# A new fixed order of attention, weight decoding and first MLP, with no tensor operation on GpSimd

## Chip, core and metric

The kernel runs on one core of one Trainium2 chip. The metric is the device time of one execution in microseconds (us), as the median of several runs; less is better. The profiles are of one execution each, taken by the hardware profiler, and times within it count from the span's start.

## What is computed

Chunked attention, an MLP with a swish, and a mixture of eight experts with one expert for each token, all in float32, on 2 x 768 tokens of 512 dimensions. Cut to what matters:

```python
for c in range(nc):                       # chunks of 32 queries
    k_full = concat([mem_k, k[:, :, l_start:r_end]])   # 8 + up to 56 keys
    a = exp(s - max(s)); a = a / (a.sum(-1) + 1e-9)    # s = scale * q_c @ k_full.T
    out[:, :, c_start:c_end] = a @ v_full
h = x @ w_in                              # first MLP: 512 -> 2048 -> 512
x = (h / (1 + exp(-1.702 * h))) @ w_out
logits = x @ w_gate                       # second: the best of 8 experts
y = relu(x_e @ w1[e]) @ w2[e]             # at most 384 tokens of each, 512 -> 1024 -> 512
out = gate_w * y
```

The weights of the first MLP come in 64 bits. The kernel decodes them from pairs of 32-bit words.

## The kernel before

Tokens are in 12 groups of 128, two groups to a block of the first MLP. All products of the MLPs are made from values split in a high and a low part, with three matmuls for each product (high by high, high by low, low by high).

The first part of the program is issued in an order written out by hand, the string ORDER. Each word is a step, a letter and a number. The scheduler keeps this order on each engine (`in_order`), and an engine's instruction that waits holds all behind it on that engine. The last step of the string is followed by a loop over the rest of the first MLP with the routing, and then by the experts. Those two parts are generated by the program and scheduled by priorities.

Steps of a group g of attention: Q, K, V load (SyncE's queue; two buffers each); c makes the scores (TensorE, 64 small matmuls, line 424); m the maximum (VectorE, 444); s the difference (VectorE, 451); x the exponential (ScalarE, 456), X that of two groups at once; r the sum (VectorE, 460); q adds a small number (463) and i takes the reciprocal (466, both VectorE); n divides on VectorE, N on GpSimd (470); d transposes (TensorE, 477); p copies with zeros beside (ScalarE, 485); e multiplies with the values (TensorE, 494); h and l write the high part (ScalarE, 506) and the low part (VectorE, 509) of xT, the input of the first MLP.

Steps of a piece of weights p (32 pieces of 128 x 512; in each eight, four of w_in, then four of w_out): L loads its raw words (SyncE, three buffers, line 938); a takes the absolute value of the high words (ScalarE, 254); b limits it (258), f shifts it (261), o sets the sign (265, all VectorE); t converts the low words on ScalarE (273), T on VectorE (275); g adds the two on GpSimd, G on VectorE (279); w makes the high part (ScalarE, 284); j the low part on VectorE, J on GpSimd (289).

Steps of a unit u of the first MLP (96 units; one is a block of 256 tokens by 128 hidden columns): A makes the hidden values (TensorE, 12 matmuls, 528) into one of two PSUM buffers; z and y apply the swish twice (ScalarE, 543 and 547), which frees the buffer; u makes the low part on VectorE, U on GpSimd (551); B multiplies with w_out (TensorE, 6 matmuls, 571) into two accumulators; v adds a finished accumulator to x2 (VectorE, 584; the first twelve are copied by ScalarE, 587). Units run in four passes over the hidden columns, four columns' chunks in a pass, and within a pass over the six blocks of tokens. U1 = 74 says that ORDER holds the units below 74.

F is a number of matmuls without use, which keep the tensor engine's clock up (line 929). E ends attention: it gives back its memory.

Of the kernel before, what the change touches and what calls it, by code (L numbers as in the profile page):

```python
# [54 lines left out]
i4 z4 b8 y4 r5 N4 w6 u4 B1 z5 q5 j6 i5 m7 N5 A6 y5 f8 s7 u5 A7 o8 X7 T7 T8 c8 L10 G7 L11 r6 z6 T9 d4 a9 K10 q6
m8 d5 z7 Q10 p4 c9 r7 s8 p5 G8 B2 Q11 m9 a10 K11 w8 T10 e4 s9 w7 j8 y6 J7 b10 e5 V6 q7 f10 i7 U6 o10 X9 B3 i6
V7 G10 N6 h5 n7 h4 c10 r8 v1 v0 l4 q8 l5 d6 B4 i8 m10 y7 p6 b9 U7 n8 A8 w10 f9 r9 a11 J10 A9 o9 z8 y8 b11 L12
g9 q9 i9 A10 L13 f11 z9 o11 U8 w9 B5 t11 N9 j9 z10 L14 g11 d7 y9 d8 t12 s10 A11 p7 u9 a12 e6 z11 b12 t13 f12
a13 B6 o12 V8 a14 b13 L15 h6 b14 w11 B7 l6 y10 j11 p8 U10 e7 f14 f13 y11 v3 o14 U11 v2 e8 G12 V9 h7 o13 w12 l7
B8 a15 V10 j12 h8 L16 G13 A12 l8 w13 T14 t15 A13 j13 L17 z12 y12 G14 U12 b15 A14 w14 f15 z13 j14 d9 o15 t16 B9  # L60
a16 L18 G15 p9 b16 B10 T17 f16 y13 z14 U13 o16 w15 e9 a17 L19 G16 y14 j15 a18 A15 b17 V11 h9 b18 t18 f17 f18
B11 z15 o17 o18 L20 g17 a19 c11 l9 L21 v4 y15 b19 g18 v5 T19 f19 A16 u15 m11 A17 o19 t20 u14 L22 g19 s11 z16
B12 z17 T21 B13 X11 B14 r10 r11 B15 y16 q10 y17 i10 q11 U16 i11 u17 N10 A18 v6 v7 N11 d10 z18 B16 y18 p10 U18
d11 e10 p11 A19 h10 l10 e11 z19 y19 U19 B17 h11 l11 B18 E0 w16 w17 j16 w18 A20 j17 w19 a20 j18 J19 B19 a21 b20
z20 b21 y20 f20 a22 A21 U20 f21 v8 b22 v9 o21 A22 f22 z21 g21 y21 o20 o22 L23 A23 z22 g20 L24 y22 u22 A24 U21
T22 w20 L25 G22 w21 z23 j20 B20 J21 z24 y23 t23 a23 A25 U23 y24 b23 w22 U24 T24 a24 A26 f23 J22 o23 z25 a25
b24 L26 B21 g23 f24 z26 b25 o24 B22 w23 f25 L27 G24 y25 t25 u25 B23 y26 o25 U26 a26 T26 L28 j23 g25 A27 v11
b26 v10 f26 w24 T27 A28 o26 z27 J24 y27 a27 L29 G26 A29 w25 b27 U27 t28 f27 J25 z28 o27 B24 a28 z29 L30 b28
w26 g27 f28 B25 y28 o28 a29 J26 T29 w27 L31 A30 u28 y29 b29 u29 f29 A31 j27 a30 G28 z30 b30 B26 t30 o29 z31
a31 f30 g29 B27 o30 y30 b31 U30 T31 A32 v12 y31 g30 v13 A33 f31 z32 U31 o31 G31 B28 z33 B29 y32 U32 A34 y33  # L70
U33 A35 z34 B30 z35 B31 y34 u34 A36 v14 y35 v15 A37 u35 z36 B32 z37 B33 y36 u36 A38 y37 U37 A39 z38 B34 z39
B35 y38 u38 A40 v17 y39 U39 v16 A41 z40 B36 z41 B37 y40 u40 B38 y41 u41 A42 A43 z42 y42 U42 B39 z43 A44 v19
y43 v18 A45 u43 z44 B40 z45 B41 y44 U44 A46 y45 u45 A47 z46 B42 z47 w28 w29 J28 B43 y46 w30 u46 w31 J29 A48
v21 y47 v20 J31 A49 z48 J30 B44 U47 B45 y48 z49 U48 A50 y49 U49 A51 z50 B46 z51 B47 y50 u50 A52 v23 y51 u51
# [1124 lines left out]
```

## Time and profile before

| | |
|---|---|
| time, median of 3 runs | 566.86 us (565.52 to 567.95) |
| the profiled execution: its span, first to last instruction | 564.0 us |
| its span below the median of the runs | 2.9 us |
| TensorE matmul busy | 525.7 us, 93% of the span |
| VectorE | 309.0 us, 55% |
| ScalarE | 272.1 us, 48% |
| GpSimd | 139.0 us, 25% |
| mean granted clock of TensorE | 0.979 of full speed |

Of the profiled execution the page gives the span alone; the runs of the table are other executions. The engines PE, PEld, DVE, ACT, POOL and SP of the profile are TensorE's matmuls, its weight loads, VectorE, ScalarE, GpSimd and SyncE. A busy share is a mean over parts of the program that are bound by different engines. A duration is from start to end of an instruction; successive instructions of an engine can overlap a little, so the distance of starts is the pace.

### The profile page before, as it was taken

How to read it: one execution, taken by the hardware profiler on the slowest of the kernel's cores; microseconds unless marked ns; L12 is line 12 of the kernel's file. 1: busy time of each engine (PE TensorE's matmuls, PEld its weight loads, DVE VectorE, ACT ScalarE, POOL GpSimd, SP SyncE). 2: the span in 40 equal slices, each digit the busy share in tenths (PEclk: the TensorE clock that was granted, in tenths of full speed). 3: DMA queues.
4: the chain of work that ended last, by engine and by line, in shares of the span. 5: the costliest groups of instructions: out<-in, count | busy, mean ns of one | idle time of the engine just before them, and what ended most of it. 6: DMA issues, size and time to landing. Idle time of an engine off the chain costs nothing.

```text
span 564.0 us, 10773 instructions
## 1 busy us (share of the span) xinstructions
PE 525.7 (93%) x4266; PEld 452.3 (80%) x4272; DVE 309.0 (55%) x580; ACT 272.1 (48%) x543; POOL 139.0 (25%) x147
## 2 busy tenths in 40 slices
PE   8599799999699999999999999939999999999995
PEld 4498578797588989898998888528998898899894
DVE  4999999669962111212237344525846082975350
ACT  3588977766532242222145333216654282956250
POOL 3543341537540050201100000150040214302011
PEclk9889999999899999999999999969999999999998
DMA  8857756304450000000028511386957165895100
GB/s 322 321 180 266 248 170 230 127 21 151 134 181 0 1 1 1 1 1 0 1 71 279 175 39 40 114 277 215 299 178 266 58 205 184 275 371 184 72 26 29
DMA packets 39036, 80.57 MB, mean 143 GB/s; under 512 B 4025, under 2 KB 10169, under 8 KB 38970
## 3 DMA queue, kind: packets, MB, share of 16 engines
q1 hardware_dynamic: 36010, 70.66, 37.1%
q0 software_dynamic: 2960, 9.01, 5.1%
q8 instruction: 44, 0.72, 0.5%
q14 instruction: 22, 0.18, 0.1%
HBM read 70.16 MB, written 10.27 MB: 143 GB/s over the span
## 4 chain that ended last, share of the span: by engine, by line
PE 56%; DVE 17%; issue 13%; DMA 7%; ACT 5%; POOL 1%; POOLq 0%; SPq 0%; ACTq 0%
PE acc L571 18%; PE psh L528 17%; PE psy L816 8%; PE psh L750 6%; DVE w L258 3%; DVE w L265 3%; DMA out_dram<-y,taker 2%; DVE w L289 2%; PE psh L772 2%; DVE w L261 2%; DMA out_dram<-y,tl 2%; DVE rest L275 1%; DMA kt<-in_k_dram 1%; PE psr L598 1%; DVE xT L509 1%
## 5 line engine op out<-in xcount | busy, mean ns | idle before, releaser
L528 PE MATMUL psh<-xT,w 128*128 128x256 f32 x1152 | 153.1, 287 | 14.2 <-ACT g L547 7.5
L528 PEld LDWEIGHTS psh<-xT,w 128*128 128x128 f32 x1152 | 146.6, 193 | 22.1 <-ACT g L547 10.1
L571 PE MATMUL acc<-w,g 128*128 128x512 f32 x576 | 148.0, 400 | 2.5 <-DVE x L584 0.9
L571 PEld LDWEIGHTS acc<-w,g 128*128 128x128 f32 x576 | 103.4, 188 | 25.9 <-issue 2.1
L289 DVE TENSOR_TENSOR w<-raw,w 128x1024 fp32r<-128x1024 f32 x64 | 77.1, 1217 | 48.9 <-ACT w L284 48.7
L816 PE MATMUL psy<-w,hT 128*128 128x512 f32 x360 | 87.5, 398 | 0.3 <-ACT y L836 0.3
L543 ACT ACTIVATE sg<-psh 128x256 f32<-128x256 f32 x96 | 36.7, 383 | 100.2 <-PE psh L528 95.8
L551 DVE TENSOR_TENSOR g<-sg,g 128x256 fp32r<-128x256 f32 x57 | 28.1, 494 | 99.6 <-ACT g L547 92.7
L816 PEld LDWEIGHTS psy<-w,hT 128*128 128x128 f32 x360 | 66.5, 188 | 16.3 <-ACT y L836 0.6
L750 PEld LDWEIGHTS psh<-xs,w 128*128 128x128 f32 x576 | 69.0, 188 | 0.6
L750 PE MATMUL psh<-xs,w 128*128 128x256 f32 x576 | 69.2, 281 | 0.0
L284 ACT ACTIVATE w<-raw 128x1024 fp32r<-128x1024 f32 x64 | 66.4, 1062 | 0.0
L551 POOL TENSOR_TENSOR g<-sg,g 128x256 fp32r<-128x256 f32 x39 | 32.8, 841 | 114.4 <-ACT g L547 109.6
L547 ACT ACTIVATE g<-psh 128x256 fp32r<-128x256 f32 x96 | 36.6, 382 | 35.3 <-PE acc L571 35.1
L699 POOL DMA_INDIRECT xr<-rows,taker x22 | 26.7, 1216 | 98.3 <-issue 97.5
L584 DVE SCALAR_TENSOR_TENSOR x<-acc,x 128x512 f32<-128x512 f32 x36 | 23.5, 684 | 25.5 <-PE acc L571 25.5
L279 POOL TENSOR_TENSOR w<-w,rest 128x512 int32<-128x512 int32 x17 | 24.7, 1458 | 28.4 <-DVE w L265 27.4
L837 POOL DMA_INDIRECT out_dram<-y,taker x7 | 7.0, 1004 | 92.1 <-ACTq L854 71.9
L289 POOL TENSOR_TENSOR w<-w,w 128x512 fp32r<-128x512 f32 x16 | 22.5, 1413 | 26.4 <-ACT w L284 25.9
L265 DVE SCALAR_TENSOR_TENSOR w<-raw,w 128x512 int32<-128x512 int32 x32 | 26.9, 852 | 0.3
L284 ACT ACTIVATE w<-w 128x512 fp32r<-128x512 f32 x32 | 19.4, 627 | 12.3 <-POOL w L279 8.1
L772 PE MATMUL psh<-w,xs 128*128 128x512 f32 x72 | 19.4, 421 | 5.8 <-issue 5.8
(108 smaller groups left out, 503.2 us busy)
## 6 DMA issues: line engine op xcount, KB each, us to landing
raw<-in_w_dram SPq DMA_DIRECT2D x64, 512.0 KB, 5.8
raw<-in_w_in_dram SPq DMA_DIRECT2D x16, 512.0 KB, 4.2
raw<-in_w_out_dram SPq DMA_DIRECT2D x16, 512.0 KB, 3.6
vt<-in_v_dram SPq DMA_DIRECT2D x12, 512.0 KB, 6.2
...
```

What stands on the lines that cost most here:

```text
L265: nc.vector.scalar_tensor_tensor(out=self.w, in0=self.words()[1], scalar=-0x40000000, in1=self.w, op0=ALU.bitwise_and, op1=ALU.bitwise_or)
L284: nc.scalar.activation(out=w_dst(self.name, self.i, 0), in_=w, func=AF.Copy)
L289: eng.tensor_tensor(out=lo, in0=w, in1=hi.bitcast(F32), op=ALU.subtract)
L528: nc.tensor.matmul(ps, lhsT=w[:, wz, c, i * P:(i + 1) * P], rhs=xT[tb][:, xz, c, :], start=n == 0, stop=n == 3 * KC - 1)
L543: nc.scalar.activation(out=sg_t[u], in_=h_t[u], func=AF.Silu, scale=1.702)
L547: g_last[:1] = [nc.scalar.activation(out=g[:, 0], in_=h_t.pop(u), func=AF.Silu, scale=1.702).ins]
L551: lo = eng.tensor_tensor(out=g[:, 1], in0=sg_t.pop(u), in1=g[:, 0].bitcast(F32), op=ALU.subtract)
L571: nc.tensor.matmul(acc_t[tb][s], lhsT=g[:, gz, s * P:(s + 1) * P], rhs=w[:, wz, i, :], start=i == 0 and n == 0, stop=i == QF - 1 and n == 2)
L699: return nc.gpsimd.indirect_dma_start(out=t, out_offset=None, in_=rows[:, :], in_offset=bass.IndirectOffsetOnAxis(ap=taker[:, b, e:e + 1], ...
L750: mm = nc.tensor.matmul(ps, lhsT=w[:, wz, c, f0:f0 + P], rhs=t[:, xz, c, :], start=m == 0, stop=m == 3 * KC - 1)
L772: nc.tensor.matmul(p1[j], lhsT=x[:, xz, c, o:o + P], rhs=w[:, wz, c, :], start=(xz, wz, c) == (0, 0, 0), stop=(xz, wz, c) == (1, 0, KC - 1))
L816: nc.tensor.matmul(ps, lhsT=h[:, hz, fc, o:o + P], rhs=w[:, wz, fc % 4, :], start=fc == 0 and n == 0, stop=fc == F2 - 1 and n == 2)
```

## The change

The string ORDER is replaced by another of the same kind. A constant PASSES and a list of units take the place of the division of a unit's number into pass, block and column. Comments are left out everywhere. Counted in the two strings:

| steps | before | after |
|---|---|---|
| n on VectorE / N on GpSimd | 3 / 9 | 12 / 0 |
| x of one group / X of two | 2 / 5 | 12 / 0 |
| t on ScalarE / T on VectorE | 15 / 17 | 24 / 8 |
| G on VectorE / g on GpSimd | 15 / 17 | 32 / 0 |
| j on VectorE / J on GpSimd | 16 / 16 | 32 / 0 |
| u on VectorE / U on GpSimd | 35 / 39 | 74 / 0 |
| matmuls of the F steps | 42 | 70 |
| changes between exponential and swish on ScalarE | 10 | 6 |
| before A0: c / l / pieces with a low part on either engine | 4 / 2 / 3 | 6 / 4 / 3 |
| pieces with a low part before A20, A30, A38 | 17, 27, 28 | 15, 22, 27 |

All other steps are there as often as before. The diff, cut:

```diff
+PASSES = (4, 4, 4, 4)
...
 ORDER = """
-Q0 K0 Q1 K1 V0 V1 L0 L1 L2 F11 c0 m0 K2 F2 c1 Q2 s0 x0 m1 Q3 K3 r0 s1 q0 x1 i0 N0 t0 r1 a0 q1 F17 d0 b0 a1 i1
-T1 N1 p0 b1 f0 f1 a2 o0 F7 d1 e0 o1 p1 L3 g0 b2 L4 f2 h0 V2 g1 F1 c2 o2 t2 l0 w0 G2 w1 e1 J0 Q4 m2 w2 K4 s2 c3
-a3 J2 V3 T3 h1 L5 b3 l1 J1 a4 Q5 m3 t4 K5 b4 F4 A0 s3 f4 X3 f3 A1 o4 o3 g4 c4 r2 L6 z0 L7 r3 y0 g3 w4 u0 A2 z1
...
+Q0 K0 V0 L2 Q1 K1 V1 F18 c0 Q2 m0 K2 s0 x0 T2 a2 r0 b2 q0 f2 F15 c1 i0 o2 n0 Q3 G2 d0 K3 m1 L1 p0 s1 w2 F4 e0 x1
+j2 c2 V2 h0 r1 l0 c3 Q4 q1 m2 K4 L0 i1 s2 a1 Q5 K5 n1 x2 t1 r2 F5 d1 m3 p1 q2 s3 F4 e1 i2 x3 b1 n2 c4 V3 h1 r3
+L3 a0 l1 d2 t0 q3 f1 p2 i3 o1 F4 c5 n3 L5 G1 e2 m4 w1 b0 V4 h2 j1 a3 l2 t3 s4 f0 F9 d3 x4 m5 a5 r4 p3 o0 q4 L4
+G0 F6 e3 i4 w0 s5 V5 h3 n4 Q6 x5 K6 l3 F3 d4 t5 j0 p4 r5 F2 A0 b3 a4 q5 f3 e4 i5 o3 n5 A1 L6 z0 V6 h4 G3 Q7 y0
...
+u27 B25 w30 f17 b23 z28 t23 j30 A29 y28 o17 a31 u28 L25 B26 G17 z29 y29 f23 w17 u29 A30 o23 t31 j17 L29 B27 G23
...
+    unit_list = [(k, tb, i, sum(PASSES[:k]) + i)
+                 for k, n in enumerate(PASSES) for tb in range(NTB) for i in range(n)]
+    last_use = {fc // QF: u for u, (_, _, _, fc) in enumerate(unit_list)}
...
+    def last_of(k, tb):
+        return NTB * sum(PASSES[:k]) + (tb + 1) * PASSES[k] - 1
...
     def stage2(u, alone=True):
-        j, tb, i = unit_of(u)
+        _, tb, i, _ = unit_of(u)
         g = g_t.pop(u)
-        w = w_tile(("wo", j), i)
...
-        if i < QF - 1:
-            return
-        if tb == NTB - 1 and s == SUB - 1:
+        if u == last_use[j] and s == SUB - 1:
             w_free(("wo", j))
-        if alone:
+        if alone and u == last_of(k, tb):
             keep_x2(u, s)
```

## Rows read from the trace of the kernel before

**Rows 1.** The page's slices: busy tenths of each of 40 equal slices.
```profile
DVE  4999999669962111212237344525846082975350
...
POOL 3543341537540050201100000150040214302011
```

**Rows 2.** Stages: length, each engine's busy us (count), TensorE's clock, DMA share, GB/s.
```profile
0.00:24.20 24.20, 18.55 (x367) 11.15 (x371) 16.23 (x30) 11.58 (x19) 11.03 (x19) 1.00 0.85 311
24.20:162.20 138.00, 121.16 (x1448) 105.18 (x1448) 126.74 (x212) 98.03 (x187) 62.79 (x53) 0.96 0.54 185
162.20:280.40 118.20, 118.14 (x744) 106.07 (x745) 25.79 (x49) 32.45 (x85) 19.22 (x23) 1.00 0.01 2
280.40:564.00 283.60, 267.83 (x1710) 229.88 (x1711) 140.28 (x293) 130.07 (x253) 45.92 (x53) 0.98 0.51 167
```

**Rows 3.** Single lines: duration in ns, min/median/max; first and last start.
```profile
L258 DVE TENSOR_SCALAR w<-w x32: 410/420/1524, 12.8 to 159.2; 128x512 f32<-128x512 f32 x32
...
L451 DVE TENSOR_TENSOR pp<-pss,mx x12: 675/680/691, 7.3 to 104.2; 128x512 f32<-128x512 f32 x12
```

**Rows 4.** VectorE's timeline: start, us, instruction.
```profile
33.39 0.19 DVE L466 RECIPROCAL rs<-rs 128x8 f32<-128x8 f32 x1
33.51 0.59 DVE L463 TENSOR_SCALAR rs<-rs 128x8 f32<-128x8 f32 x1
...
39.40 0.42 DVE L258 TENSOR_SCALAR w<-w 128x512 f32<-128x512 f32 x1
39.74 0.68 DVE L451 TENSOR_TENSOR pp<-pss,mx 128x512 f32<-128x512 f32 x1
40.34 0.41 DVE L261 TENSOR_SCALAR w<-w 128x512 int32<-128x512 int32 x1
...
41.00 0.68 DVE L265 SCALAR_TENSOR_TENSOR w<-raw,w 128x512 int32<-128x512 int32 x1
41.61 0.42 DVE L261 TENSOR_SCALAR w<-w 128x512 int32<-128x512 int32 x1
```

**Rows 5.** The chain that ended last, in the dense stage: start, us, what.
```profile
168.17 2.79 PE acc L571 x12
170.96 2.82 PE psh L528 x24
```

**Rows 6.** TensorE's waits, 24.2 to 162.2: us in total, times, longest.
```profile
PE psh L528 <- ACT g L547: 7.5, 6, 4.4
```

**Rows 7.** TensorE's timeline at four steps of attention.
```profile
35.99 0.60 PE L477 MATMUL psd<-ident,pp 128*128 128x128 f32 x4
36.52 1.10 PE L424 MATMUL pss<-kt,qt 64*32 64x64 f32 x64
37.55 0.66 PE L477 MATMUL psd<-ident,pp 128*128 128x128 f32 x4
...
39.56 2.08 PE L494 MATMUL pse<-apart,vt 128*64 128x64 f32 x64
41.58 2.33 PE L424 MATMUL pss<-kt,qt 64*32 64x64 f32 x128
```

**Rows 8.** The timeline of the start, up to A0.
```profile
0.78 4.51 PE L929 MATMUL spare<-const-bfloat16-1.0 128*128 128x512 bf16 x11 [0.78 <-PEq L1183]
...
5.22 1.10 PE L424 MATMUL pss<-kt,qt 64*32 64x64 f32 x64
...
6.58 0.69 DVE L444 TENSOR_REDUCE mx<-pss 128x8 f32<-128x512 f32 x1
...
9.14 3.66 PE L929 MATMUL spare<-const-bfloat16-1.0 128*128 128x512 bf16 x16 [0.16 <-issue]
...
24.18 0.38 PE L528 MATMUL psh<-xT,w 128*128 128x256 f32 x1 [2.58 <-ACT xT L506]
```

**Rows 9.** The timeline around one wait of TensorE.
```profile
148.39 0.67 ACT L273 ACTIVATE rest<-raw 128x512 int32<-128x512 uint32 x1 [3.86 <-DVE w L279]
...
151.00 4.63 PE L528 MATMUL psh<-xT,w 128*128 128x256 f32 x24 [4.37 <-ACT g L547]
```

More of the change, by code (lines that the diff above doesn't have):

```diff
@@ L55 @@
[L55 to L74, printed above, removed]
@@ new lines @@
+j2 c2 V2 h0 r1 l0 c3 Q4 q1 m2 K4 L0 i1 s2 a1 Q5 K5 n1 x2 t1 r2 F5 d1 m3 p1 q2 s3 F4 e1 i2 x3 b1 n2 c4 V3 h1 r3
+L3 a0 l1 d2 t0 q3 f1 p2 i3 o1 F4 c5 n3 L5 G1 e2 m4 w1 b0 V4 h2 j1 a3 l2 t3 s4 f0 F9 d3 x4 m5 a5 r4 p3 o0 q4 L4
+G0 F6 e3 i4 w0 s5 V5 h3 n4 Q6 x5 K6 l3 F3 d4 t5 j0 p4 r5 F2 A0 b3 a4 q5 f3 e4 i5 o3 n5 A1 L6 z0 V6 h4 G3 Q7 y0
+l4 d5 K7 w3 A2 u0 z1 j3 p5 b5 c6 b4 z2 f5 y1 f4 y2 A3 Q8 t4 u1 K8 u2 a6 o5 e5 z3 o4 L7 y3 A4 G5 V7 h5 u3 w5 l5
+c7 t6 j5 z4 G4 A5 Q9 b6 K9 w4 m6 L9 c8 z5 j4 a7 f6 B0 t7 b7 o6 f7 L13 y4 B1 G6 u4 w6 o7 A6 y5 j6 L8 Q10 u5 a9 B2
@@ new lines @@
+K10 G7 z6 s6 w7 A7 m7 t9 j7 y6 a13 u6 c9 s7 z7 t13 m8 A8 a8 m9 s8 B3 z8 s9 v0 b9 c10 b13 y7 f9 v1 u7 A9 o9 f13
+G9 x6 B4 x7 r6 x8 r7 x9 B5 q6 q7 w9 i6 i7 n6 t8 n7 B6 r8 r9 z9 d6 y8 B7 q8 q9 y9 u8 p6 u9 i8 i9 A10 n8 v2 n9 v3
+e6 j9 z10 y10 o13 A11 V8 h6 u10 L18 G13 L16 B8 l6 w13 Q11 K11 b8 z11 j13 y11 d7 B9 u11 p7 f8 m10 o8 B10 s10 a18
+G8 e7 t18 b18 w8 f18 B11 V9 h7 T16 j8 L12 a16 l7 d8 v4 d9 o18 v5 A12 p8 b16 L11 G18 c11 f16 p9 o16 A13 z12 L19
+G16 y12 m11 a12 e8 u12 z13 s11 t12 A14 b12 V10 y13 T11 h8 u13 a11 B12 l8 z14 f12 y14 b11 A15 u14 o12 x10 f11 L10
@@ new lines @@
+B13 G12 x11 r10 w12 e9 r11 t19 q10 q11 B14 i10 i11 V11 h9 n10 l9 d10 n11 A16 z15 j12 p10 o11 d11 z16 e10 L15 G11
+y15 y16 u15 A17 p11 u16 T10 h10 B15 z17 l10 w11 y17 j11 A18 v6 u17 v7 e11 z18 y18 A19 u18 h11 l11 E0 w18 B16 w16
+j18 z19 j16 a19 A20 y19 b19 a10 u19 f19 a15 B17 b10 z20 o19 y20 f10 L20 A21 u20 G19 o10 B18 w19 b15 z21 L14 t15
+j19 A22 y21 G10 a20 u21 f15 B19 w10 b20 o15 z22 v8 A23 j10 L22 y22 v9 u22 G15 t20 B20 f20 z23 T14 w15 o20 A24
+y23 a14 u23 L30 j15 a22 B21 G20 z24 y24 b14 w20 u24 A25 f14 t22 j20 B22 o14 z25 a30 b22 L17 G14 y25 A26 u25 w14
@@ new lines @@
+f22 t30 j14 B23 z26 o22 y26 v10 b30 L23 A27 u26 v11 G22 a17 f30 B24 w22 b17 o30 z27 t17 j22 A28 L31 y27 G30 a23
+u27 B25 w30 f17 b23 z28 t23 j30 A29 y28 o17 a31 u28 L25 B26 G17 z29 y29 f23 w17 u29 A30 o23 t31 j17 L29 B27 G23
+z30 y30 b31 w23 u30 A31 v12 a25 v13 t25 j23 B28 z31 f31 a29 b25 y31 A32 o31 u31 L28 G31 B29 z32 f25 w31 b29 o25
+y32 A33 t29 u32 L21 j31 B30 G25 z33 a28 f29 T28 y33 A34 o29 u33 L24 G29 B31 a21 b28 z34 v14 w29 A35 f28 y34 v15
+t21 u34 B32 j29 z35 y35 o28 A36 u35 L27 G28 b21 w28 B33 T24 z36 j28 y36 f21 A37 u36 o21 L26 G21 B34 z37 y37 T27
@@ new lines @@
+w21 u37 A38 j21 B35 z38 y38 v16 A39 u38 v17 B36 z39 y39 u39 A40 B37 z40 y40 u40 A41 B38 z41 y41 u41 A42 B39 z42
+y42 v18 A43 u42 v19 B40 z43 y43 u43 A44 B41 z44 y44 u44 A45 B42 z45 y45 u45 A46 B43 z46 y46 v20 A47 u46 v21 B44
+z47 w25 y47 j25 A48 u47 a24 a27 B45 b24 f24 z48 b27 a26 o24 A49 y48 u48 G24 B46 z49 f27 w24 b26 o27 y49 A50 t26
+u49 j24 B47 G27 z50 y50 f26 w27 u50 A51 v22 v23 j27 B48 z51 o26 y51 u51 A52 G26 w26 B49 z52 j26 y52 u52 A53 B50
+z53 y53 u53 A54 B51 z54 y54 v24 A55 u54 v25 B52 z55 y55 u55 A56 B53 z56 y56 u56 A57 B54 z57 y57 u57 A58 B55 z58
@@ L80 @@
+y58 v26 A59 u58 v27 B56 z59 y59 u59 A60 B57 z60 y60 u60 A61 B58 z61 y61 u61 A62 B59 z62 y62 v28 A63 u62 v29 B60
+z63 y63 u63 A64 B61 z64 y64 u64 A65 B62 z65 y65 u65 A66 B63 z66 y66 v30 A67 u66 v31 B64 z67 y67 u67 A68 B65 z68
+y68 u68 A69 B66 z69 y69 u69 A70 B67 z70 y70 v32 A71 u70 v33 B68 z71 y71 u71 A72 B69 z72 y72 u72 A73 B70 z73 y73
+u73 B71 v34 v35
 """
@@ L119 @@
     QF = NFC // NQ
+    assert sum(PASSES) == NFC and PASSES[-1] == QF
     F2 = F // P
@@ L514 @@
     acc_t = {}
+    unit_list = [(k, tb, i, sum(PASSES[:k]) + i)
+                 for k, n in enumerate(PASSES) for tb in range(NTB) for i in range(n)]
+    last_use = {fc // QF: u for u, (_, _, _, fc) in enumerate(unit_list)}
     def unit_of(u):
-        j, r = divmod(u, NTB * QF)
-        tb, i = divmod(r, QF)
-        return j, tb, i
+        return unit_list[u]
+    def last_of(k, tb):
+        return NTB * sum(PASSES[:k]) + (tb + 1) * PASSES[k] - 1
     def stage1(u, alone=True):
-        j, tb, i = unit_of(u)
+        _, tb, _, fc = unit_of(u)
+        j, i = divmod(fc, QF)
         w = w_tile(("wi", j), i)
@@ L530, in stage1 @@
                 n += 1
-        if tb == NTB - 1 and i == QF - 1:
+        if u == last_use[j]:
             w_free(("wi", j))
@@ L567, in stage2_group @@
     def stage2_group(u, s, g, alone=True):
-        j, tb, i = unit_of(u)
-        w = w_tile(("wo", j), i)
+        k, tb, i, fc = unit_of(u)
+        j, wi = divmod(fc, QF)
+        w = w_tile(("wo", j), wi)
         for n, (gz, wz) in enumerate(((0, 0), (0, 1), (1, 0))):
-            nc.tensor.matmul(acc_t[tb][s], lhsT=g[:, gz, s * P:(s + 1) * P], rhs=w[:, wz, i, :],
-                             start=i == 0 and n == 0, stop=i == QF - 1 and n == 2)
-        if i < QF - 1:
-            return
-        if tb == NTB - 1 and s == SUB - 1:
+            nc.tensor.matmul(acc_t[tb][s], lhsT=g[:, gz, s * P:(s + 1) * P], rhs=w[:, wz, wi, :],
+                             start=i == 0 and n == 0, stop=u == last_of(k, tb) and n == 2)
+        if u == last_use[j] and s == SUB - 1:
             w_free(("wo", j))
-        if alone:
+        if alone and u == last_of(k, tb):
             keep_x2(u, s)
     def keep_x2(u, s):
-        j, tb, i = unit_of(u)
+        k, tb, _, _ = unit_of(u)
         dst = x2[:, tb * SUB + s, :DM]
-        if j > 0:
+        if k > 0:
             nc.vector.scalar_tensor_tensor(out=dst, in0=acc_t[tb][s], scalar=1 / 1.702, in1=dst, op0=ALU.mult,
@@ L968 @@
             A=lambda u: stage1(u, False), z=unit_act, y=unit_hi, u=lambda u: unit_lo(u, nc.vector),
-            U=lambda u: unit_lo(u, nc.gpsimd), B=lambda u: stage2(u, False), v=lambda a: keep_x2(a // SUB * QF + QF - 1, a % SUB),
+            U=lambda u: unit_lo(u, nc.gpsimd), B=lambda u: stage2(u, False), v=lambda a: keep_x2(last_of(*divmod(a // SUB, NTB)), a % SUB),
             E=after_attention)
@@ L1015 @@
                     stage2(u - LAG)
-                    j2, tb2, i2 = unit_of(u - LAG)
-                    if j2 == NQ - 1 and i2 == QF - 1:
+                    k2, tb2, _, _ = unit_of(u - LAG)
+                    if k2 == len(PASSES) - 1 and u - LAG == last_of(k2, tb2):
                         gs = list(range(tb2 * SUB, (tb2 + 1) * SUB))
```

8 lines of the change are left out of this document (removed).

## The prediction

> **What bounds the kernel now.** I read the page's forty slices first, then a table by stage, then the rows of single instructions, and last the waits of the stage that is not dense. In the slices [rows 1] the reader is to see VectorE near full for the first eleven, and GpSimd busy in the same ones. The table by stage [rows 2] is cut at three places: at 24.2 us, where the first matmul of the first MLP (unit A0) starts [rows 8], at 162.2, and at 280.4, where unit 74 starts, the first that the written order does not hold; the ledger below bears that place out.
>
> The dense stage, 162.2 to 280.4, is TensorE alone: 118.14 of 118.2 us busy [rows 2]. Two A steps (24 matmuls) start 2.82 us before what follows them, two B steps (12 matmuls) 2.79 [rows 5], so A is 1.41 and B 1.40. From A34 on the order has 40 A and 44 B left: 40 x 1.41 + 44 x 1.40 = 118.0, the stage to 0.2 us. Nothing is to be had there, except by starting it earlier.
>
> The stage before it, 24.2 to 162.2, is VectorE's: 126.74 of 138 us busy, with GpSimd busy for 62.8 [rows 2]. VectorE's operations are stretched there. The 512-column maximum of line 258 has a median of 420 ns and a longest of 1524; the sum of 8 columns of line 463 once took 0.59 us [rows 4]; but the subtraction of line 451, which reads PSUM, never passes 691 ns [rows 3]. Beside no GpSimd work the starts follow each other by 0.34 us (lines 258, 261, 275, 551) or 0.60 to 0.61 (lines 265, 279, 289, 444, 451, 460, 470, 509, 584) [rows 4]; the reported durations, 0.41 and 0.68, overlap by the difference. The small steps q and i come to 0.2 us together (0.12 between line 466 and what follows it [rows 4], and less for q, an estimate from it). At that pace the VectorE steps between A0 and A33 (8 m, 9 s, 3 n, 10 l, 28 o, 13 G, 16 j, 2 v at 0.61; 10 r at 0.60; 10 q and i; 27 b, 28 f, 15 T, 12 u at 0.34) come to 54.3 + 6.0 + 2.0 + 27.9 = 90.2 us; they took 126.7. So some 36 us of VectorE's stage are stretch, 10 more are waiting.
>
> TensorE's own ledger follows. A step of scores takes 1.03 us and one of transposes about 0.53 (the starts at 35.99, 36.52 and 37.55), one of values 1.01 (two between 39.56 and 41.58) [rows 7]. From A0 on, the order before has 8 c, 10 d, 10 e, 74 A and 72 B: 8.2 + 5.3 + 10.1 + 104.3 + 100.8 = 228.7 us. It took 280.4 - 24.2 = 256.2. The loss after A0 is 27.5 us, all of it before 162.2. Of it 138.0 - 121.2 = 16.8 are idle [rows 2], 7.5 of them for ScalarE's g [rows 6]; the rest is slow running, as in the matmuls from 151.00, where 24 took 4.63 us for 2.82 after a wait of 4.37 [rows 9], with the granted clock of the whole stage at 0.96 [rows 2].
>
> So the span is 24.2 (until A0) + 228.7 (TensorE's work) + 27.5 (loss) + 283.6 (all behind unit 74) = 564.0 us. The profiled execution's span lies 2.9 us under the median of the runs, 566.86, and I add that to every sum.
>
> **The change part by part.** PASSES of four fours gives the same list of units as the old division by 24 and 4, the same last uses and the same places for v: those edits move nothing (that part of the change does not do anything here), and the loops behind unit 74 emit what they did. I price them and the last 283.6 us at no change; there VectorE, ScalarE and the loads are those of before, and no written step is left over.
>
> *GpSimd's work comes to VectorE.* Counted in the two orders: 9 divisions n, 17 additions g, 16 lo parts j at 0.61 and 39 lo parts u at 0.34, less 9 rest steps that go to ScalarE: 42 x 0.61 + 39 x 0.34 - 9 x 0.34 = 35.8 us more, 125.9 to 161.7 in all. What leaves is the stretch of 36 us. In total VectorE is even; the gain must come from place. 27 decoded pieces stood before A30, now 22, and 27 only before A38; and most of the 39 u lie after 162.2, where VectorE was 25.8 us busy of 118.2 [rows 2]. They are covered by TensorE's matmuls; without that cover they would cost 13.3 us.
>
> The stretch that the rows show is on operations whose inputs are all in SBUF. The Trainium skill (SBUF — State Buffer, "Who interferes with whom") says that VectorE and GpSimd lock one shared port pair for a whole instruction, and that a VectorE operation with at most one SBUF input outside the two-port modes does not contend; the rows of lines 258 and 451 agree with it. By that rule alone, all 36 us of stretch would go.
>
> *The start.* 18 fills stand before the first scores where 11 stood. Eleven took 4.51 us, 0.41 each [rows 8], so 18 take 7.4 and the scores start at 0.8 + 7.4 = 8.2, not 5.2; if the last seven run at the 0.23 of the sixteen at 9.14 [rows 8], at 6.9. I take 8.2, as no fill ran faster ahead of the first scores. The maximum follows 1.36 us behind the scores' start [rows 8]: VectorE starts at 9.5 (bound 8.3). Fifteen more fills (3.5 us) before the second scores hide behind T2, r0, b2, f2, o2, n0 and G2 on VectorE, and that order also holds V0 and L2 ahead of K1 in SP's queue. In all 28 more fills, 6.4 us at 0.23, lie before A0; TensorE has 14.2 us of other work there in almost 30 us, so they cost nothing but the first seven.
>
> *A0 comes later.* Six groups' maxima, four l and three finished pieces stand before it, where four, two and three did, and all of it is VectorE's now: its steps before A0 (6 m, 6 s, 5 n, 4 l, 3 o, 3 G, 3 j at 0.61; 6 r at 0.60; 5 q and i; 3 b, 3 f, 1 T at 0.34) are 18.3 + 3.6 + 1.0 + 2.4 = 25.3 us; before, by the same count, they were 12.9. Before, VectorE idled some 2 of the 17.6 us between its first maximum and A0 (16.2 busy, an estimated 0.6 of it earlier) [rows 2, 8]; the same share gives 3.2. A0 starts at 9.5 + 25.3 + 3.2 = 38.0, against 24.2: 13.8 later. Bound from below, without idling and with the fast fills: 33.6. SP's loads before A0 grow from 9.1 to 10.8 MB; at the 311 GB/s of the first stage [rows 2] they need 34.7 us, so they fit, barely.
>
> *TensorE from A0 on.* 6 c, 7 d, 8 e, 74 A, 72 B: 6.2 + 3.7 + 8.1 + 104.3 + 100.8 = 223.1. It has 5.6 us less to do, since attention went ahead.
>
> *The loss after A0.* Here is the gain. From A0 to A38 VectorE has 103 us of steps in 122 us of TensorE's work, 85%; before, with the stretch, it was the longer of the two. Had VectorE's queue to set when the rest of TensorE's work can follow, unit 74 would come, counted in the same way, at these times. At A8: 9.5 + 3.2 + 45.3 + 200.9 (TensorE's work from A8) = 258.9; at l7: 9.5 + 3.2 + 65.5 + 178.6 = 256.8; at A38: 9.5 + 3.2 + 128.5 + 102.6 = 243.8. TensorE's own sum is 38.0 + 223.1 = 261.1. TensorE leads by 2 to 4 us until l7 and by more later. That is little to absorb the waits of queues in order, so I don't take the loss at nothing; it lies between 0 and the old 27.5, and I take 5, near the lower end, because the lateness that caused the old one was stretch. ScalarE changes table 6 times for 10, and carries 9 more rest steps; it was 98 of 138 us busy [rows 2] and stays behind VectorE, so that is priced at nothing, and the 4 loads saved are cover if it is not.
>
> Sum: 38.0 + 223.1 + 5 + 283.6 = 549.7, 14.3 less; with 2.9 a median of 552.6 us.
>
> **The rivals.** *Slower: decoding at the head of the queues.* B lies some three units behind A, but A has only two PSUM buffers, freed by ScalarE's z and y. In the order before, a rest step on ScalarE waited 3.86 us for VectorE, y stood behind it, and TensorE waited 4.37 [rows 9]. The new order puts all additions and lo parts, which ScalarE's t and w wait for, into one queue with u. If the whole old loss of 27.5 stays, A0's 13.8 us of delay are on top: 38.0 + 223.1 + 27.5 + 283.6 = 572.2, median 575. It decides from a loss of 19.3, where the gain is gone; at 22 the run is slower by 0.5%. For it: VectorE at 85% in an order fixed by hand leaves each of its waits to the others. Against it: VectorE was at 92% and had stretched steps when those waits arose [rows 2, 9].
>
> *No change: the stretch is not GpSimd's doing.* VectorE would keep its 36 us to A38: 9.5 + 3.2 + 128.5 + 36 + 102.6 = 279.8, median 566.3. [Rows 3] speak against it. The Trainium skill (Perfetto Trace Analysis, "Optimizing Scalar/DVE Operations") says that a saturated VectorE may be helped by handing work to GpSimd, which is the reverse of this change, and adds that between those two it might not help; no run here yet shows which of the two halves holds.
>
> *No change: A0 starved of loads.* If the 10.8 MB come at the 185 GB/s of the second stage [rows 2], A0 waits until 58.4, and even without a loss the sum is 565.1, median 568.0. Against it: 185 was demand, not a limit, since buffers of two and three set the starts.
>
> *More gain:* no loss and A0 at 33.6: 540.3, median 543.2.
>
> **How the numbers follow.** The forecast (loss up to 12, with the case of more gain) has 0.77, the slower rival 0.13, the unchanged stretch 0.04, starved loads 0.06. The likeliest case has 552.6, with its own range 543 to 560. Below 543.5 I leave 0.05 and above 566 about 0.15, so the range is 543.5 to 566. Half a per cent, 2.8 us, is about what a measurement of this kernel can tell from no change: faster 0.78 (loss under 16.5), same 0.08, slower 0.14.
>
> **What would show it.** Right: A0 near 38; line 258 and line 551 with a longest near their medians; no GpSimd tensor work before unit 74; VectorE under 90% busy from 40 to 160, TensorE dense from about 40 to 50 us; unit 74 near 266; the stage behind it at 283.6. Wrong: TensorE waits for ScalarE's g or VectorE's xT above 15 us in sum between 38 and 150, ScalarE waiting for VectorE in front of y, or a VectorE that idles for loads before A0. A last stage off by more than 2 us would break the sum in a place that I priced at nothing.

## The result, and the profile after

The changed kernel takes 549.97 us (median of 4, 548.52 to 553.03), the kernel before, run beside it, 566.65: a ratio of 0.971, 95% interval 0.968 to 0.974. The forecast was 552.6 within 543.5 to 566. The profiled span is 548.5 us, the mean granted clock 0.989.

The slices of the page, then four stretches, cut at the new A0, at 162.2 as before, and at the new unit 74 (columns as in [rows 1, 2]; the third spans A0 to unit 74):

```profile
PE   8799999999999999999999999679999999999995
...
DVE  4978989698972362322275445327573182966350
...
POOL 2000000000000000000000000411121306201111
```
```profile
0.00:36.60 36.60, 30.04 (x597) 18.80 (x603) 25.49 (x58) 18.55 (x31) 3.48 (x13) 1.00 0.75 265
36.60:162.20 125.60, 125.59 (x1349) 112.19 (x1348) 108.54 (x232) 93.58 (x192) 0.00 (x0) 1.00 0.50 171
36.60:263.60 227.00, 226.99 (x1991) 203.49 (x1989) 143.33 (x303) 121.75 (x272) 0.00 (x0) 1.00 0.31 104
263.60:548.50 284.90, 268.87 (x1709) 230.36 (x1709) 140.92 (x293) 129.23 (x251) 46.19 (x53) 0.98 0.50 166
```

From A0 to unit 74 TensorE is busy 226.99 of 227.00 us at a granted clock of 1.00 (2.4 GHz), and its table of waits is empty there. Before, the first 138 us of that stage held 16.8 us of idling, at a granted clock of 0.96 [rows 2]. GpSimd has no tensor work between A0 and unit 74. The instructions that the stretch was read from now show no stretch (columns as in [rows 3]):

```profile
L260 DVE TENSOR_SCALAR w<-w x32: 374/419/427, 10.2 to 193.0; 128x512 f32<-128x512 f32 x32
...
L453 DVE TENSOR_TENSOR pp<-pss,mx x12: 639/682/691, 8.2 to 88.3; 128x512 f32<-128x512 f32 x12
...
L561 DVE TENSOR_TENSOR g<-sg,g x96: 415/425/428, 41.5 to 334.1; 128x256 fp32r<-128x256 f32 x96
```

L260 is the maximum, line 258 before: its longest fell from 1524 ns to 427. L453 is the subtraction that reads PSUM, line 451 before; its 691 did not move.

The start, in TensorE's and VectorE's timeline (start, us, instruction, in brackets the idle time before it and what ended it; cf. [rows 8]):

```profile
0.79 5.41 PE L937 MATMUL spare<-const-bfloat16-1.0 128*128 128x512 bf16 x18 [0.79 <-PEq L1191]
6.13 1.10 PE L426 MATMUL pss<-kt,qt 64*32 64x64 f32 x64
7.48 0.69 DVE L446 TENSOR_REDUCE mx<-pss 128x8 f32<-128x512 f32 x1
...
27.62 0.75 PE L426 MATMUL pss<-kt,qt 64*32 64x64 f32 x37 [1.23 <-issue]
28.30 1.15 PE L496 MATMUL pse<-apart,vt 128*64 128x64 f32 x32
30.13 0.69 DVE L511 TENSOR_TENSOR xT<-pse,xT 128x512 fp32r<-128x512 f32 x1 [2.33 <-ACT xT L508]
...
36.46 0.68 DVE L291 TENSOR_TENSOR w<-w,w 128x512 fp32r<-128x512 f32 x1
36.60 2.06 PE L538 MATMUL psh<-xT,w 128*128 128x256 f32 x12
38.58 1.15 PE L496 MATMUL pse<-apart,vt 128*64 128x64 f32 x32
...
263.60 1.58 PE L538 MATMUL psh<-xT,w 128*128 128x256 f32 x12
```

A0 starts at 36.6 and unit 74 at 263.6, so the prediction's ledger reads 36.6 + 223.1 + 3.9 + 284.9 = 548.5, beside 38.0 + 223.1 + 5 + 283.6 = 549.7 in the forecast.

### The profile page after: what moved, and what is told of

Read it like the earlier page. It is cut to its first block, busy times and chain, and to the rows that moved or that the text cites. A ratio compares the mean times of both kernels' runs of the same rounds, so it can differ in the third digit from the quotient of the medians.

```text
span 548.5 us, 10788 instructions
## 1 busy us (share of the span) xinstructions
PE 525.9 (96%) x4292; PEld 452.6 (83%) x4300; DVE 309.7 (56%) x652; ACT 269.5 (49%) x553; POOL 49.7 (9%) x66
## 4 chain that ended last, share of the span: by engine, by line
PE 77%; issue 11%; DMA 6%; DVE 2%; POOL 1%; ACT 1%; SPq 0%; POOLq 0%; ACTq 0%
PE psh L538 25%; PE acc L581 25%; PE psy L824 8%; PE psh L758 6%; PE psh L780 3%; DMA out_dram<-y,taker 2%; PE pse L496 2%; PE pss L426 2%; DMA out_dram<-y,tl 2%; PE spare L937 1%; DMA kt<-in_k_dram 1%; PE psr L606 1%; POOL xr L707 1%; DMA xr<-rows,taker 1%; PE psd L479 1%
## 5 line engine op out<-in xcount | busy, mean ns | idle before, releaser
L538 PEld LDWEIGHTS psh<-xT,w 128*128 128x128 f32 x1152 | 148.2, 189 | 7.5 <-DVE w L291 0.2
L581 PE MATMUL acc<-w,g 128*128 128x512 f32 x576 | 151.7, 398 | 0.0
L581 PEld LDWEIGHTS acc<-w,g 128*128 128x128 f32 x576 | 101.3, 188 | 20.0 <-issue 2.1
L561 DVE TENSOR_TENSOR g<-sg,g 128x256 fp32r<-128x256 f32 x96 | 40.4, 423 | 84.6 <-ACT g L557 81.6
L937 PE MATMUL spare<-const-bfloat16-1.0 128*128 128x512 bf16 x95 | 24.9, 397 | 1.7 <-issue 0.8
L291 DVE TENSOR_TENSOR w<-w,w 128x512 fp32r<-128x512 f32 x32 | 21.9, 686 | 3.9 <-ACT w L286 3.6
L780 PEld LDWEIGHTS psh<-w,xs 128*128 128x128 f32 x72 | 14.9, 214 | 10.8 <-issue 7.6
L256 ACT ACTIVATE w<-raw 128x512 f32<-128x512 f32 x32 | 21.2, 673 | 3.8 <-DMA raw<-in_w_in_dram 3.3
L844 ACT ACTIVATE y<-psy,gt 128x512 f32<-128x512 f32 x7 | 4.8, 688 | 35.2 <-PE psy L824 35.2
```

Source lines behind the costliest of these rows:

```text
L291: eng.tensor_tensor(out=lo, in0=w, in1=hi.bitcast(F32), op=ALU.subtract)
L538: nc.tensor.matmul(ps, lhsT=w[:, wz, c, i * P:(i + 1) * P], rhs=xT[tb][:, xz, c, :], start=n == 0, stop=n == 3 * KC - 1)
L561: lo = eng.tensor_tensor(out=g[:, 1], in0=sg_t.pop(u), in1=g[:, 0].bitcast(F32), op=ALU.subtract)
L581: nc.tensor.matmul(acc_t[tb][s], lhsT=g[:, gz, s * P:(s + 1) * P], rhs=w[:, wz, wi, :], start=i == 0 and n == 0, stop=u == last_of(k, tb) ...
L780: nc.tensor.matmul(p1[j], lhsT=x[:, xz, c, o:o + P], rhs=w[:, wz, c, :], start=(xz, wz, c) == (0, 0, 0), stop=(xz, wz, c) == (1, 0, KC - 1))
L937: return nc.tensor.matmul(spare[0], lhsT=one.to_broadcast([P, P]), rhs=one.to_broadcast([P, 512]), start=True, stop=True)
```

## The experiments

Every kernel ran with the kernel before beside it, and the ratio is to that; the kernel before had medians of 567.25 (beside e1 to e4), 567.07 (beside e5 to e9) and 568.01 (beside e10 to e12). "Loss at A24" is the start of A24 less that of A0 and less TensorE's work between them at the prediction's prices; "whole loss" is the same up to unit 74. Labels are shortened to their first part.

| kernel | median us | ratio, 95% | A0 | loss at A24 | whole loss | unit 74 | behind it |
|---|---|---|---|---|---|---|---|
| before | 567.25 | 1 | 24.2 | 17.4 | 27.5 | 280.4 | 283.6 |
| after | 549.97 | 0.968–0.974 | 36.6 | 3.3 | 3.9 | 263.6 | 284.9 |
| e1: new order, GpSimd back | 550.67 | 0.968–0.972 | 37.2 | 3.4 | 6.2 | 266.5 | 284.5 |
| e2: old order, all VectorE | 556.58 | 0.979–0.983 | 22.3 | 16.5 | 18.9 | 269.9 | 285.6 |
| e3: late u on GpSimd | 551.70 | 0.969–0.974 | 41.0 | | 4.0 | 268.1 | 282.8 |
| e6: old order, last pieces later | 566.71 | 0.997–1.001 | 23.5 | 18.3 | 27.4 | 279.6 | 285.6 |
| e10: old order, last pieces spread | 559.06 | 0.982–0.987 | 24.2 | 17.5 | 19.1 | 272.0 | 284.4 |
| e11: e10, all VectorE | 553.13 | 0.971–0.975 | 22.3 | 15.1 | 15.5 | 266.5 | 284.5 |

**The two parts by themselves: order, and engine.** Of n, g, j and u the capital or small letter says whether the step runs on GpSimd or VectorE (G and g the other way round). The first kernel keeps the new order and gives GpSimd the 39 U, 16 J, 17 g and 9 N that it had:

```diff
-... c1 i0 o2 n0 Q3 G2 ... F4 c5 n3 L5 G1 e2 ... A3 Q8 t4 u1 K8 u2 ...
+... c1 i0 o2 N0 Q3 G2 ... F4 c5 N3 L5 g1 e2 ... A3 Q8 t4 U1 K8 U2 ...
```

> The new order with GpSimd given back what it had in the old one: the same 9 divisions, 17 additions, 16 low parts of pieces and 39 low parts of units, at the new order's places. My theory: the gain comes from VectorE's queue being free of stretch, so the loss after A0 comes back in part. 23 of the 39 low parts of units and 37 of the 42 others lie before A38, so VectorE's steps there fall from 128.5 to 98.1 us, and the stretch (up to 36 us) and GpSimd's longer operations (1.2 to 1.5 us for 0.6) come on top: line 260 with a longest above 1.2 us, TensorE's waits after A0 above 5 us, a span 5 to 15 us above the 548.5 of the new order. Rival: the order alone makes the gain, and then the span stays within 2 us of 548.5.

The second keeps the old order and gives every such step to VectorE:

```diff
-... x1 i0 N0 t0 r1 ... L3 g0 b2 L4 ... w1 e1 J0 Q4 ... K6 w3 U1 i2 ...
+... x1 i0 n0 t0 r1 ... L3 G0 b2 L4 ... w1 e1 j0 Q4 ... K6 w3 u1 i2 ...
```

> The old order with the same steps on VectorE that the new order has there: no tensor operation on GpSimd in the ordered part. My theory: the stretch of 36 us goes and 29.7 us of steps before A33 come to VectorE (38 at 0.61, 19 at 0.34), so its queue sets the dense stage's start at about 6.6 + 132.7 + 13 of waiting = 152 us for 162: a span of about 554, faster than 564.0 by 6 to 14. All of line 258's durations near 0.42 us. Rival (the order makes the gain, the engine none): 564 or more, since the old order has all its decoding early and VectorE gets more of it.

With GpSimd back in the new order the stretch is back and the time is not. The lines of that kernel (one less than the changed kernel's), then its stages and its one wait of TensorE for VectorE's x:

```profile
L259 DVE TENSOR_SCALAR w<-w x32: 377/420/1524, 11.5 to 196.2; 128x512 f32<-128x512 f32 x32
...
L560 DVE TENSOR_TENSOR g<-sg,g x57: 409/425/1341, 42.5 to 337.0; 128x256 fp32r<-128x256 f32 x57
L560 POOL TENSOR_TENSOR g<-sg,g x39: 726/742/2514, 44.7 to 259.1; 128x256 fp32r<-128x256 f32 x39
...
L452 DVE TENSOR_TENSOR pp<-pss,mx x12: 640/686/692, 9.5 to 89.4; 128x512 f32<-128x512 f32 x12
```
```profile
0.00:36.60 36.60, 30.46 (x591) 18.34 (x598) 21.02 (x48) 17.72 (x29) 13.65 (x22) 1.00 0.75 262
36.60:162.20 125.60, 124.02 (x1335) 110.13 (x1336) 103.20 (x178) 92.02 (x191) 58.10 (x50) 1.00 0.50 167
```
```profile
PE acc L580 <- DVE x L591: 1.6, 1, 1.6
```

From 36.6 to 162.2 us GpSimd does 58.10 us of work there, and VectorE, with 54 instructions fewer (178 for 232), is busy only 5.3 us less, 103.20 for 108.54. The rest it pays back in stretch: the maximum's longest is 1524 ns again, while the subtraction from PSUM stays at 692. So the reading of the stretch was right. The theory on record, 5 to 15 us more, was not; its rival, the order alone, came nearest, with a span of 551.0 for 548.5. VectorE is not the longer queue in this order, and the stretch is covered: its 2.3 us of added loss, 1.6 of them in that one wait, leave 550.67 beside 549.97, with overlapping ranges. In the old order the same exchange is worth 10.7 us; the same stretch of time in that kernel:

```profile
36.60:162.20 125.60, 118.53 (x1329) 103.22 (x1328) 110.88 (x243) 91.85 (x178) 0.00 (x0) 0.99 0.53 176
```

TensorE is busy 118.53 of these 125.6 us, for 110.98 in the kernel before, and it waits, between 25 and 265 us, most for the same two as there, ScalarE's g [rows 6] and VectorE's xT (us in total, times, longest):

```profile
PE psh L527 <- ACT g L546: 3.7, 5, 1.2
...
PE psh L527 <- DVE xT L508: 2.1, 2, 1.2
```

The two parts by the medians:

| | GpSimd share | all on VectorE | difference |
|---|---|---|---|
| old order | 567.25 | 556.58 | 10.7 |
| new order | 550.67 | 549.97 | 0.7, not resolved |
| difference | 16.6 | 6.6 | |

(Three of the four ran side by side; the changed kernel's 549.97 is from its own group, where the kernel before had 566.65.) The order alone gives 16.6 us. The prediction's cause of the gain falls: taking GpSimd off gives 10.7 us in the old order, but the gain does not need it.

**GpSimd late.** Behind A38 VectorE is idle for more than half of the time (34.79 of 100.6 us busy from 163 us to unit 74), so the change's choice should not matter there. The 36 u behind A38 go back to GpSimd:

```diff
-... A39 u38 v17 B36 z39 y39 u39 A40 B37 z40 y40 u40 ...
+... A39 U38 v17 B36 z39 y39 U39 A40 B37 z40 y40 U40 ...
```

> The new order with the 36 low parts of units behind A38 on GpSimd. Theory: there VectorE is busy for about a quarter to half of the time and TensorE has the queue of three units ahead, so a low part of 0.74 us for 0.42 and some stretch are covered: within 1 us of the new order's 550.0 median. Rival: GpSimd costs wherever it works, by its stretch of the 10 pieces that are still decoded then: 2 us or more slower.

The median is 551.70, the interval overlaps that of the changed kernel, and the loss is 4.0 for 3.9: nothing. The profile holds a surprise all the same, A0 at 41.02 with the code ahead of it unchanged:

```profile
0.78 6.81 PE L936 MATMUL spare<-const-bfloat16-1.0 128*128 128x512 bf16 x18 [0.78 <-PEq L1190]
...
30.73 1.28 PE L425 MATMUL pss<-kt,qt 64*32 64x64 f32 x37 [2.33 <-issue]
...
41.02 1.23 PE L537 MATMUL psh<-xT,w 128*128 128x256 f32 x5
```

The 18 fills took 6.81 us for 5.41, and a break of TensorE within c5 2.33 for 1.23. Behind that break the granted clock is 0.50 from 30.3 to 33.6 us; behind its shorter break the changed kernel has 1.00. The fills differ in pace; they are told apart here by window, first in the changed kernel, then in e3 (duration in ns, min/median/max; first and last start):

```profile
L937 PE MATMUL spare<-const-bfloat16-1.0 x6: 584/631/631, 0.8 to 2.9; 128*128 128x512 bf16 x6
L937 PE MATMUL spare<-const-bfloat16-1.0 x11: 379/381/382, 3.6 to 5.8; 128*128 128x512 bf16 x11
```
```profile
L936 PE MATMUL spare<-const-bfloat16-1.0 x6: 582/631/631, 0.8 to 2.9; 128*128 128x512 bf16 x6
L936 PE MATMUL spare<-const-bfloat16-1.0 x7: 631/631/631, 3.3 to 5.9; 128*128 128x512 bf16 x7
L936 PE MATMUL spare<-const-bfloat16-1.0 x5: 380/381/434, 6.3 to 7.2; 128*128 128x512 bf16 x5
```

The slow ones start 0.43 us apart, the fast ones 0.22. Six are slow in the changed kernel (with one between) and thirteen in e3. So a profile's A0 scatters by up to 4.4 us by itself, and the kernels that change the start have to be read with that in mind.

**What the order does: 1. Where the last pieces are decoded.** In the old order the loss grows by 17.4 us up to A24 and by 9.9 from there to A34, then no more. In that second stretch stand most decode steps of pieces 24 to 31. First they are all moved 14 units later, in the same density:

```diff
-... A24 U21 T22 w20 L25 G22 ... U24 T24 a24 A26 f23 J22 o23 z25 a25 b24 L26 B21 ...
+... A24 U21 T22 w20 G22 ... U24 A26 f23 J22 o23 z25 B21 ...
```

> The old order, GpSimd's share kept, with one thing moved: the steps of the last eight pieces (24 to 31), which stood between A23 and A36, come fourteen units later. In the old kernel the loss after A0 grows by 9.9 us between A24 and A34 and by nothing later. Theory (the order's gain is that VectorE has less to do for each unit of TensorE's work while TensorE is not yet ahead): that growth goes, TensorE is dense from A24, and the span falls by 7 to 10 us, to 554 to 557. Rival 1 (the gain of the new order is attention that is ahead): no change, 564. Rival 2: the loss comes back fourteen units later, because GpSimd stretches VectorE wherever decoding is: no change.

566.71, no change: the loss grows by 1.2 instead of 9.9 between A24 and A40 and then, with the moved steps, to 23.3 at A42, 26.4 at A46 and 27.4 at A56. The windows of that kernel:

```profile
150.00:160.00 10.00, 10.00 (x69) 9.13 (x68) 1.39 (x2) 2.79 (x8) 2.95 (x4) 1.00 0.01 2
...
170.00:180.00 10.00, 8.16 (x50) 7.14 (x49) 7.08 (x13) 3.96 (x9) 2.02 (x2) 0.98 0.23 68
180.00:190.00 10.00, 10.00 (x55) 8.58 (x53) 7.49 (x12) 6.13 (x13) 5.87 (x5) 0.85 0.36 113
190.00:200.00 10.00, 7.60 (x49) 6.50 (x49) 9.97 (x15) 3.91 (x10) 4.63 (x4) 1.00 0.79 265
```

The stretch from 150 to 160, inside the old lossy one, is dense now. Where the heap stands, VectorE is busy 7.08, 7.49 and 9.97 of 10 us; TensorE idles 1.8 us in the first and 2.4 in the last, and between them runs at a granted clock of 0.85. From 165 to 210 us it waits 3.1 us for VectorE's x and 1.5 for ScalarE's g. Later is no remedy: of what was expected, the second rival held.

Next the same steps are spread, each at 1.9 times its distance from A23 (that is, up to A48), with GpSimd's share kept:

```diff
-... y25 t25 u25 B23 y26 o25 U26 a26 T26 L28 j23 g25 A27 ...
+... y25 u25 B23 y26 ... A28 T24 z27 a24 y27 A29 a25 b24 U27 L26 z28 f24 B24 b25 ...
```

> The old order, GpSimd's share kept, with the steps of the last eight pieces spread over 24 units (A23 to A48) instead of 13. When they were moved fourteen units later in one heap, the loss between A24 and A40 was 1.2 us for 9.9, but 7.9 us came back between A40 and A52. Theory, now: what costs is the heap, in which VectorE (with stretch) needs longer than TensorE; spread, VectorE's 21 us of net steps and the stretch on them have 67 us of TensorE's work to hide behind. So the loss stays near 19 after A24, the span near 556 (554 to 559). Rival: a piece costs TensorE about 1 us wherever it is decoded beside GpSimd: 564 again.

559.06, 8.9 us less than beside it. A window of 38 us (A24 to A34 of the kernel before) in the kernel before, then in this one:

```profile
127.00:165.00 38.00, 31.08 (x183) 26.80 (x182) 37.14 (x48) 19.61 (x44) 23.61 (x19) 0.96 0.52 171
```
```profile
127.00:165.00 38.00, 37.39 (x242) 33.24 (x241) 29.29 (x39) 20.28 (x47) 19.99 (x18) 1.00 0.33 110
```

VectorE falls from 37.14 of 38 us to 29.29 and TensorE rises from 31.08 to 37.39. The loss stays at 19 from A34 on. With stretch and GpSimd's work left in, spreading a fourth of the pieces gives 8.9 us, as the theory on record had it.

Last, both remedies in the old order, the spread one of above with e2's replacement:

```diff
-... x1 i0 N0 t0 r1 ... L3 g0 b2 L4 ... w1 e1 J0 Q4 ...
+... x1 i0 n0 t0 r1 ... L3 G0 b2 L4 ... w1 e1 j0 Q4 ...
```

> The last run's order with all tensor steps on VectorE. On VectorE alone the old order had a loss of 16.5 us at A24 and 18.8 at the end. Theory: spreading has only the 2.2 us behind A24 left to take, so the span is 552 to 554 (555.5 without the spreading), and the two remedies, GpSimd's removal and the spreading, overlap behind A24. Rival: they add, and the span falls to 548 or below.

553.13. The gains of 10.7 (no GpSimd) and 8.9 (spread), each against the kernel before beside it, come to 14.9 together, not to their sum of 19.6: they relieve in part the same heap. Behind A24 the loss is now 0.4. Up to A24 it is still 15.1.

**What the order does: 2. The start.** Four kernels shorten the changed kernel's way to A0: 11 fills for 18, the load V2 behind K5 in SP's queue, the values e2 ahead of the scores c5, and all three together.

```diff
-... V1 F18 c0 ...
+... V1 F11 c0 ...
-... j2 c2 V2 h0 ... Q5 K5 n1 ...
+... j2 c2 h0 ... Q5 K5 V2 n1 ...
-... F4 c5 n3 L5 G1 e2 m4 ...
+... F4 e2 c5 n3 L5 G1 m4 ...
```

> The new order with 11 instead of 18 matmuls of fill ahead of the first scores. In the new kernel the 18 took 5.34 us until the scores at 6.13, so the last seven ran at 0.23 us or less; 11 let the scores start at about 5.3. Theory: A0 waits for VectorE, which starts with the first maximum, so A0 and the end come 0.8 us earlier. Rival 1: the loads of the groups 4 and 5 set A0, and nothing moves. Rival 2: the granted clock is not yet up without the seven, and the first scores and fills run slower: up to 1 us later.

> The new order with one load moved: V2 is issued behind K5, not ahead of Q4. In the new kernel the scores of group 4 and 5 waited for their keys' loads and in two profiles of the same start A0 came at 36.6 and 41.0. Theory: the loads of the start set a part of A0's time, the keys come some 1.7 us earlier (0.5 MB at 311 GB/s), and A0 and the end 1 to 2 us earlier. Rival: A0 is set by VectorE's steps alone, or V2 is now the late one: no change within 0.5 us.

> The new order with e2 ahead of c5 on TensorE. In the new kernel c5 ran from 25.78 to 28.3 with a break of 1.23 us, e2 stood behind it, and VectorE was idle for 2.33 us for the high part that follows e2. Theory: that idle time goes, and A0 and the end come about 2 us earlier. Rival: c5's delay moves on to m5 and r5 behind it, and A0 stays: no change.

> The new order with the three small changes of the start together: 11 fills first, V2 behind K5, e2 ahead of c5. Theory: A0 at 33 to 34.5 for 36.6, since VectorE's idle time ahead of it falls, and 2 to 4 us less at the end, a median of 546 to 548: it beats both kernels. Rival: TensorE is no longer the longer queue from A0 on, and an earlier A0 is lost again as waits behind it; then A0 comes earlier and the loss after it grows from 3.5 us by as much.

| kernel | median us (range) | A0 | whole loss |
|---|---|---|---|
| 11 fills | 551.80 (549.27–553.07) | 35.8 | 3.9 |
| V2 later | 551.08 (549.79–553.76) | 36.8 | 4.5 |
| e2 first | 549.75 (548.36–552.66) | 35.7 | 4.1 |
| all three | 548.80 (547.90–550.26) | 35.2 | 4.1 |

None is resolved from 549.97 (548.52 to 553.03). The forecast for all three, A0 at 33 to 34.5 and a median of 546 to 548, was missed. A0 moves by at most 1.4 us, well inside its own scatter of 4.4. In the last kernel the three changes stay, pieces 0 and 2 exchange their places, and the units A0 and A1 stand where fills stood:

```diff
-... t3 s4 f0 F9 d3 x4 m5 ... L4 G0 F6 e3 i4 w0 ... r5 F2 A0 b3 ... n5 A1 L6 ...
+... t3 s4 f2 A0 d3 x4 m5 ... L4 G2 A1 e3 i4 w2 ... r5 F2 b3 ... n5 L6 ...
```

> The three small changes of the start, and A0 and A1 put where two groups of fills (9 and 6) stood, with the steps of the pieces 0 and 2 exchanged so that A0's weights come first. In the new kernel A0 waited for the low part of piece 0, decoded third. Theory: TensorE gains 2.8 us of work done in the time of the fills, and A2, which VectorE's steps allow at about 40 us, comes 1 to 3 us earlier: a median of 546 to 548, the fastest of all. Rival: A2 waits for z0 and y0, which stand behind the exponential of group 5 on ScalarE, and keeps its time: 548.8 as without.

Its units A0, A1 and A2 in TensorE's timeline, and a line of ScalarE's:

```profile
27.51 1.68 PE L537 MATMUL psh<-xT,w 128*128 128x256 f32 x12
...
29.38 1.65 PE L537 MATMUL psh<-xT,w 128*128 128x256 f32 x12
...
39.11 2.58 PE L537 MATMUL psh<-xT,w 128*128 128x256 f32 x12 [0.18 <-ACT g L556]
```
```profile
36.62 1.28 ACT L552 ACT_TABLE_LOAD   x1
```

A0 and A1 now start at 27.5 and 29.4; A2, at 39.1, was released last by ScalarE's g, which stood behind a table load of 1.28 us at 36.62, and its twelve matmuls took 2.58 us, at a granted clock of 0.50 (37.8 to 41.1 us) after waits of 0.89, 1.24 and 0.72 us. A2 is 2.4 us earlier than in the changed kernel, A8 1.5, unit 74 1.5. The median, 548.69 (546.59 to 549.90), is the lowest of all, but its ratio of 0.964 to 0.969 touches the changed kernel's: 1.3 us by the medians, more by the ratios, since the kernel before beside it was slower (568.01 for 566.65). It is not resolved, and above the 546 to 548 expected.

## Why the prediction came out

**Right, by the size of the terms.** A0 came at 36.6 for 38.0; TensorE's work from there is the priced 223.1 in both; the loss was 3.9 for 5; the stage behind unit 74 284.9 for 283.6. The span is 1.2 us under the sum, and the median of the runs lies 1.5 us above the span for 2.9 before, which makes the 2.6 us between 552.6 and 549.97. Seen in the profile as forecast: A0 near 38, TensorE dense from it on, unit 74 near 266, no tensor work on GpSimd, the medians and longest of the maximum and u alike, VectorE at 104.02 of 120 us (87%) between 40 and 160.

**The loss term came near by luck.** Its 5 us were set for "the waits of queues in order". No such wait was there: TensorE was busy 226.99 of 227.00 us, at a granted clock of 1.00. The 3.9 are TensorE's steps above their prices. A0 alone has 0.6 of it, as the step behind it starts 1.98 us later (36.60, 38.58) for a price of 1.41; most of the rest comes by 0.1 to 0.2 us where a step of attention follows a unit's, all before A20, and by some 0.02 us for a unit.

**The failed step is the reason for the loss term**: "the lateness that caused the old one was stretch". With the stretch back in the new order the loss is 6.2, not 27.5. The stretch was real and GpSimd's doing (1524 ns with it and 427 without, in one and the same order, which ends the rival of the unchanged stretch; the Trainium skill's rule on the shared ports, SBUF — State Buffer, "Who interferes with whom", agrees), and in the old order it carries 8.6 us of the loss, 27.5 to 18.9. But it does so only together with the place of the pieces. The loss from A24 to unit 74, by the table:

| pieces 24 to 31 | with stretch | without |
|---|---|---|
| in a heap | 10.1 (before) | 2.4 (e2) |
| spread | 1.6 (e10) | 0.4 (e11) |

Either remedy takes most of it. Ten A and ten B of TensorE's, 28.1 us at their prices, lie between A24 and A34. In the kernel before, VectorE was busy 37.14 us in the 38 that they took, as shown above. Without the stretch (e2, from its A24 to its A34) the same heap still fills VectorE, but is hardly longer than TensorE's work:

```profile
124.30:154.60 30.30, 28.73 (x183) 25.34 (x182) 29.74 (x65) 19.63 (x44) 0.00 (x0) 1.00 0.63 208
```

The prediction had the place in its hands, "the gain must come from place", with 27 pieces decoded before A30 in the old order and before A38 in the new, and then gave the gain to the stretch alone.

**The start** had errors that cancel in part. 18 fills took 5.41 us, not 7.4, as eleven of them ran at the fast pace, so the first maximum came at 7.48 for 9.5. From there to A0 VectorE was busy 24.9 us (25.3 forecast) and idle 4.2 (3.2); 2.33 of these were one wait, behind the late c5 and e2. That the same fills took 5.47 to 6.81 us in four other kernels says that the price was too high, by an amount that changes from run to run.

**The rivals.** Slower, by queues in a fixed order: TensorE waited for no engine from A0 to unit 74, so VectorE's one long queue delayed nobody who mattered. Starved loads: 265 GB/s up to A0, not 185, and A0 in time. More gain: as waiting the loss did go to nothing, the start did not reach its bound of 33.6. The Trainium skill (Perfetto Trace Analysis, "Optimizing Scalar/DVE Operations") left open whether handing VectorE's work to GpSimd helps; here, in e1 from 36.6 to 162.2 us, 58.10 us of GpSimd's work freed 5.3 us of VectorE, so it all but doesn't, and taking it back moved the time by 10.7 us in the one order and by 0.7 in the other.

**The stage behind unit 74** was priced at no change. The profiles have 282.8 to 285.6 for the same code, so the 1.3 us are inside its scatter.

**Open.** The order gives 13.0 us between the spans of the kernel before and e1 (564.0, 551.0). A24 starts 5.1 us earlier (127.1, 122.0), the way from there to unit 74 is 8.8 us shorter, and what follows is 0.9 longer. The heap of pieces 24 to 31 is most of the 8.8, as spreading it alone (e10) took 8.4 off the old loss. The 5.1 were not taken apart: the old order's loss up to A24, 15 to 18 us with or without GpSimd, stands beside an A0 that is 12 us earlier and 5.6 us more attention behind it. In the kernel before, 6.8 us of it (25.3 to 32.1) ran at a granted clock of 0.50, from within the second of two waits of TensorE, 2.58 and 2.22 us. Ahead of A24 VectorE has 105 us of steps in e2's order and 94 in the changed one (counted in the strings, at the prediction's prices), since 20 pieces have their low part by then in the one and 17 in the other; that points to the same heaping, but no run spread those earlier pieces. The differences of about 1 us between the kernels of the start stay open as well.
